# One schedule for all engines, searched anew: another order, other buffers, other ties, and four gated tiles in older buffers

## The chip, the cores and the metric

The kernel runs on one core of a Trainium2 chip. The metric is the time of one execution in microseconds (us) as the device counts it; lower is better. The core has five instruction queues: TensorE (PE, matmuls, with its weight loads shown apart as PEld), VectorE (DVE), ScalarE (ACT), GpSimd (POOL) and SyncE (SP), which only issues transfers. POOL issues some transfers as well. Each queue runs its instructions in the order in which the program puts them; queues wait for each other by semaphores.

## What is computed

Inputs are q, k and v of shape (4, 8, 768, 64) and three weight matrices. Attention picks, for each query, 6 of the chunks of 32 keys by an upper bound on the scores, and a gated layer follows.

```python
ub = sum(max(q * k_min, q * k_max))            # per query and chunk of 32 keys
ub = where(causal by chunk, ub, -1e9)
sel = the 6 chunks of largest ub, per query
scores = where(sel and causal, q @ k.T / 8, -1e9)
attn = softmax(scores) @ v                     # 8 heads, concatenated to x: (3072, 512)
gate = 1 / (1 + exp(-(x @ w_gate)))            # (3072, 1536)
out = (gate * (x @ w_val)) @ w_out             # (3072, 512)
```

## The kernel before

**Stages.** The 24 blocks of 128 rows (4 batches of 6) are dealt to eight units, u0 to u7, of three blocks each. u0 has the first blocks of batches 0 to 2, which need no choice of chunks and are computed apart ("first", names with f, as kf16_2, scf_2, expf_2_0, cmf_2_1, pvf_2_1, xf_2_1, xpsf_2_1, xTf_2_1: cast of keys, scores, exponential, causal select, values, normalised rows, their turn on PE, and its copy into xT). For u1 to u7 a stage prepares (turns q and k, takes extremes of k by chunk, bounds ub on PE, picks the sixth largest with MAX8, spreads the verdict as rows of a mask into hq), a stage attends (per head: score pieces sc on PE, exponentials exp on ACT, causal selects cm on POOL, values pv on PE, rows x on DVE), and ffn does the gated layer: 12 products g and 12 products v of 128 columns of the hidden layer each, a tanh on ACT (gate), the product of both on DVE (hg, six tiles of two column blocks a unit), then the product with w_out. In u5 to u7 part of the gate products, and in u4 to u7 the last product, are done by seven products in place of eight, with sums of blocks on DVE and POOL ahead (ss, tt, tw, sw, sx) and sums of the results on DVE behind (c11, c12, c21, c22 and so on).

**Order by hand.** Nothing in the kernel decides an order when it is built. The function declares 2010 operations with the engines on which each may run and the buffers that it reads and writes. Three long strings then fix the rest. ORDER lists all operations with an engine for each (P, A, V, G, S for PE, ACT, DVE, POOL, SP), and they are issued in that order, so each engine's own queue is the list cut down to its letter. SLOTS gives each buffer a number among those of its kind (for instance 8 banks ps of the accumulator memory, 6 tiles v, 9 tiles hg, 2 tiles osb); a buffer waits until the last user of the one that lay there before is done. TIES lists pairs a<b: operation a, on POOL, also waits for the end of operation b, on DVE, though it reads nothing of it. Durations written in the declarations (pool, dve, act, pe) were the search's input and do nothing when the kernel is built.

**Names in the prediction.** Weights come by POOL's queue as ten transfers: wgp (the first quarter of rows of the first third of w_gate's columns, L610), wg0 (the rest of that third, L612), wg1 and wg2 (the other thirds), wv0 to wv2 (L613) and wo0 to wo2 (L618). g_u0_0 to g_u0_3 read wgp and wg0, g_u0_4 to 7 read wg1, g_u0_8 to 11 read wg2. hkp... are copies of a fixed pattern into the mask rows of the keys (64 rows by 1536 columns), which may run on POOL, ACT or DVE; fl_0 to fl_29 are 30 matmuls of ones whose results nobody reads (L591). hk0/hk1 and hq0/hq1 of a unit are halves of keys and queries copied to where the score pieces read them; kx0/kx1 are the extremes (L681), kcr the ranges (L688), kt a cast of the turned keys. All plain copies stand on L452 (ACT), L454 (DVE) and L456 (POOL), the helper copy.

The lines that carry out an order:

```python
for op in plan.order():
    n = len(traced)
    op.emit(op.engine)
    for b in ties.get(op.name, ()):
        tc.add_manual_dep(traced[n], ends[b], ...)
    ends[op.name] = traced[-1].name
```

Of the kernel before, what the change touches and what calls it, by code (L numbers as in the profile page):

```python
# [108 lines left out]
qf_u1_2=V v11=G wv1=G wg1=G hq0_u1_3=G qT_u1_0=P kt_u1_3=A hk0_u1_3=G hq1_u1_3=G wv2=G xTf_2_1=A xTf_2_0=A qf_u1_0=A qm_u1_0=A
g_u0_0=P g_u0_2=P kx0_u1_3=V kcr_f=V kcr_u1=V hkp101=V hq1_u1_0=V hkf1=V kt_u1_1=V hk0_u1_1=G wg2=G qm_u1_2=A qm_u1_1=A ub_u1=P  # L110
ubn0_u1=V ubm0_u1=V hq0_u1_1=A hq0_u1_2=A g_u0_3=P g_u0_1=P mx0_u1=V ap0_u1=V apt0_u1=V hqm0_u1_0=V v_u0_1=P v_u0_0=P v_u0_2=P
hq0_u1_0=A tanh_u0_2=A tanh_u0_1=A hg_u0_1=V ubn1_u1=V v_u0_3=P tanh_u0_3=A hg_u0_3=V ubm1_u1=V hg_u0_2=V tanh_u0_0=A hg_u0_0=V
hk0_u1_0=A hq1_u1_1=A sc_u1_0_2=P exp_u1_0_2=A sc_u1_1_2=P sc_u1_0_1=P sc_u1_0_0=P exp_u1_1_2=A sc_u1_1_0=P sc_u1_1_1=P
exp_u1_0_0=A exp_u1_0_1=A v_u0_7=P wo0=G hqm0_u1_2=G sc_u1_2_2=P exp_u1_2_2=A sc_u1_2_0=P exp_u1_2_0=A sc_u1_3_0=P sc_u1_3_2=P
exp_u1_3_2=A exp_u1_1_0=A sc_u1_3_1=P exp_u1_3_1=A exp_u1_3_0=A v16_0_3=G wo1=G v_u0_4=P sc_u1_2_1=P v_u0_6=P exp_u1_2_1=A
hk1_u1_0=G v16_0_2=G wo2=G mx1_u1=V ap1_u1=V apt1_u1=V hqm1_u1_0=V g_u0_5=P tanh_u0_5=A v_u0_5=P exp_u1_1_1=A hqm1_u1_2=A g_u0_6=P
tanh_u0_6=A g_u0_7=P tanh_u0_7=A hg_u0_7=V v16_0_1=G cm_u1_3=G pv_u1_3=P cm_u1_2=G hk1_u1_1=G g_u0_4=P tanh_u0_4=A hg_u0_4=V
vf1_3=G hq1_u1_2=G pv_u1_2=P sc_u1_5_1=P sc_u1_4_2=P sc_u1_4_1=P rz_u1_1=V x_u1_1=V exp_u1_4_1=A v_u0_9=P v_u0_10=P xps_u1_1=P
xT_u1_1=A exp_u1_4_2=A hg_u0_6=V hk1_u1_3=V hg_u0_5=V v_u0_8=P g_u0_10=P tanh_u0_10=A kcr1=V hg_u0_10=V g_u0_8=P tanh_u0_8=A
hg_u0_8=V sc_u1_5_2=P exp_u1_5_2=A g_u0_9=P tanh_u0_9=A hg_u0_9=V sc_u1_4_0=P exp_u1_4_0=A cm_u1_1=G pv_u1_1=P cm_u1_0=G qn_u2_2=G  # L120
sc_u1_5_0=P pv_u1_0=P exp_u1_5_0=A sc_u1_6_1=P exp_u1_6_1=A sc_u1_6_2=P exp_u1_6_2=A exp_u1_5_1=A sc_u1_7_2=P sc_u1_7_0=P
g_u0_11=P qT_u2_2=P sc_u1_7_1=P tanh_u0_11=A exp_u1_7_2=A exp_u1_7_0=A exp_u1_7_1=A kn_u2_1=V kT_u2_1=P rz_u1_0=V x_u1_0=V
xps_u1_0=P cm_u1_5=G pv_u1_5=P cm_u1_4=G pv_u1_4=P qf_u2_2=V q1_u2=S qn_u2_1=V qT_u2_1=P sc_u1_6_0=P kt_u2_1=A exp_u1_6_0=A
kn_u2_0=G kT_u2_0=P kt_u2_0=A v_u0_11=P rz_u1_2=V xT_u1_0=V x_u1_2=V xps_u1_2=P q3_u2=S qn_u2_3=G qT_u2_3=P cm_u1_7=G pv_u1_7=P
kx0_u2_0=V o0_u0_0=P o1_u0_0=P hg_u0_11=V kx1_u2_1=V kx1_u2_0=V cm_u1_6=G pv_u1_6=P rz_u1_3=V x_u1_3=V q0_u2=S qn_u2_0=A qT_u2_0=P
o0_u0_1=P xps_u1_3=P xT_u1_3=V qf_u2_1=A hq0_u2_2=A qf_u2_3=A qm_u2_1=G hq1_u2_1=G k2_u2=S kn_u2_2=G hk1_u2_0=A xT_u1_2=A
kT_u2_2=P k3_u2=S kn_u2_3=A kT_u2_3=P qf_u2_0=V hq0_u2_1=G hq0_u2_0=G qm_u2_0=G hk0_u2_1=G o2_u0_0=P osb_u0_0=A hq1_u2_0=A
qm_u2_2=A qf0_3=S qfT_3=P o1_u0_1=P o2_u0_1=P vf_3=S kf1_3=S kf0_3=S kfT_3=P v_0_5=S v_0_4=S kx0_u2_1=V kx0_u2_3=V kx1_u2_3=V
kx1_u2_2=V kx0_u2_2=V qm_u2_3=V kcr_u2=V ub_u2=P qf16_3=V kt_u2_3=A kf16_3=V osb_u0_1=A scf_3=P expf_3_0=A out_u0_0=S vc_3=G
hk1_u2_1=G hk0_u2_0=V hk0_u2_3=G kt_u2_2=A g_u1_1=P tanh_u1_1=A hk0_u2_2=A g_u1_0=P tanh_u1_0=A o0_u0_2=P expf_3_1=A cmf_3_0=G  # L130
pvf_3_0=P o1_u0_2=P ubn1_u2=V ubn0_u2=V mx1_u2=V ap1_u2=V apt1_u2=V hqm1_u2_0=V sc_u2_4_0=P exp_u2_4_0=A sc_u2_4_2=P exp_u2_4_2=A
sc_u2_5_0=P sc_u2_5_1=P sc_u2_5_2=P exp_u2_5_2=A sc_u2_4_1=P exp_u2_4_1=A cmf_3_1=G pvf_3_1=P mx0_u2=V rzf_3_0=V ap0_u2=V xf_3_0=V
# [269 lines left out]
def kernel(  # L402
# [17 lines left out]
    T = 384  # L420
# [1036 lines left out]
```

## Time and profile before

| | us |
|---|---|
| median of three runs | 281.94 |
| lowest and highest of them | 281.69, 282.36 |
| the profiled execution | 281.46 |
| its span, first to last instruction | 279.8 |

| engine | busy us | of the span | instructions |
|---|---|---|---|
| PE | 269.8 | 96% | 2806 |
| PEld | 190.0 | 68% | 2806 |
| DVE | 232.1 | 83% | 686 |
| ACT | 180.5 | 65% | 386 |
| POOL | 163.3 | 58% | 262 |

Busy is the time in which at least one instruction of the engine runs. Matmuls overlap each other, and their ends are modelled, so PE's pace is read from the starts of its matmuls rather than from their durations. In timelines a row begins with its start and its length in us; a bracket behind a row gives the engine's idle time before it and what ended it, as far as the semaphores tell. In the view of transfers the last number is the time from issue to landing.

### The profile page before, as it was taken

The numbers are of one execution on the slowest core, as the hardware profiler recorded it, in microseconds if no ns is written. First come the engines' busy times: TensorE is split into PE (matmuls) and PEld (weight loads), VectorE is DVE, ScalarE is ACT, GpSimd is POOL, SyncE is SP. The second block draws the span as 40 slices with busy tenths as digits, with TensorE's granted clock in tenths as the row PEclk, the third lists the DMA queues.
The fourth block names the chain that finished last, engine by engine and source line by source line (L and its number), as shares of the span: only waits on it lengthen the run. The fifth ranks groups of instructions, "written<-read, shape, count | busy, mean of one in ns | idle before, by whom it ended". The sixth has DMA issues, their size and how long they took to land.

```text
span 279.8 us, 7565 instructions
## 1 busy us (share of the span) xinstructions
PE 269.8 (96%) x2806; PEld 190.0 (68%) x2806; DVE 232.1 (83%) x686; ACT 180.5 (65%) x386; POOL 163.3 (58%) x262
## 2 busy tenths in 40 slices
PE   5879999999999999999999999999999999999995
PEld 3655658667755766556687657766888688778684
DVE  4789845786998998886999987878879998888875
ACT  6178868669957943559689988997983422341430
POOL 5697744639464781633759966724766477163441
PEclk9999999999999999999999999999999999999999
DMA  6999999999999598887986230100310033000304
GB/s 161 252 264 201 211 215 204 202 184 191 180 228 189 150 177 178 177 150 134 174 144 113 60 92 16 40 0 2 74 76 2 1 82 127 2 1 2 150 2 151
DMA packets 131717, 34.70 MB, mean 124 GB/s; under 512 B 119776, under 2 KB 128736, under 8 KB 131680
## 3 DMA queue, kind: packets, MB, share of 16 engines
q1 hardware_dynamic: 126912, 29.50, 50.3%
q0 software_dynamic: 4768, 4.72, 10.2%
q8 instruction: 22, 0.36, 0.5%
q14 instruction: 15, 0.12, 0.1%
HBM read 30.67 MB, written 6.29 MB: 132 GB/s over the span
## 4 chain that ended last, share of the span: by engine, by line
PE 84%; DVE 7%; DMA 6%; issue 1%; SPq 1%; POOL 0%; DVEq 0%
PE v_u L1259 20%; PE g_u L1259 15%; PE sc_u L957 12%; PE o_u L1308 11%; PE p_u L1082 8%; PE pv_u L990 7%; DMA wg<-in_moe_w_gate_dram 5%; PE p_g_u L1191 5%; PE ube_u L896 3%; DMA kf<-in_k_dram 1%; DVE ox L1099 1%; DVE xf L768 1%; DVE sw L1099 1%; DVE kcr L681 1%; DVE kx_u L681 1%
## 5 line engine op out<-in xcount | busy, mean ns | idle before, releaser
L968 ACT ACTIVATE att_u<-sc_u 128x512 f16<-128x512 f32 (+3 forms) x184 | 86.9, 570 | 8.6 <-PE sc_u L957 7.3
L1259 PE MATMUL v_u<-xT_u,wv 128*128 128x384 f16 x384 | 72.4, 326 | 0.0
L1280 DVE SCALAR_TENSOR_TENSOR hg_u<-gate_u,v_u 128x384 f16<-128x384 f16 x96 | 51.2, 545 | 19.0 <-ACT gate_u L1271 9.4
L1271 ACT ACTIVATE gate_u<-g_u 128x384 f16<-128x384 f32 x72 | 35.1, 498 | 40.1 <-PE g_u L1259 35.0
L1259 PE MATMUL g_u<-xT_u,wg 128*128 128x384 f16 x288 | 55.9, 326 | 1.0 <-ACT xT_u L452 0.6
L1259 PEld LDWEIGHTS <-wv 128*128 128x128 f16 x384 | 36.2, 98 | 20.3 <-issue 0.2
L974 POOL TENSOR_SCALAR_AFFINE_SELECT att_u<-att_u 128x384 f16<-128x384 f16 (+1 forms) x56 | 28.1, 512 | 37.4 <-ACT att_u L968 16.5
L1259 PEld LDWEIGHTS <-wg 128*128 128x128 f16 x288 | 26.8, 98 | 18.1 <-issue 1.6
L1308 PE MATMUL o_u<-wo,hg_u 128*128 128x512 f16 x144 | 34.3, 379 | 0.0
L990 PE MATMUL pv_u<-v,att_u 128*128 128x65 f16 x640 | 26.3, 193 | 0.0
L990 PEld LDWEIGHTS <-att_u 128*128 128x128 f16 x640 | 24.2, 98 | 2.9 <-issue 0.6
L1228 DVE TENSOR_TENSOR f_g_u<-p_g_u,f_g_u 128x192 f32<-128x192 f32 (+1 forms) x72 | 25.0, 384 | 1.0 <-PE p_g_u L1191 0.4
L957 PE MATMUL sc_u<-hqe,hke 128*128 128x128 f16 (+2 forms) x220 | 25.1, 243 | 0.0
L957 PE MATMUL sc_u<-hqo,hko 128*128 128x128 f16 (+2 forms) x220 | 24.1, 243 | 0.0
L1308 PEld LDWEIGHTS <-hg_u 128*128 128x128 f16 x144 | 13.7, 98 | 13.4
L957 PEld LDWEIGHTS <-hke 128*128 128x128 f16 x220 | 16.5, 98 | 4.9 <-issue 0.6
L957 PEld LDWEIGHTS <-hko 128*128 128x128 f16 x220 | 16.4, 98 | 4.4
L673 POOL CAST v<-v 128x512 f16<-128x512 f32 x23 | 14.2, 619 | 6.3 <-DMA v<-in_v_dram 2.3
L1271 ACT ACTIVATE gate_u<-f_g_u 128x384 f16<-128x384 f32 x24 | 11.9, 519 | 5.6 <-DVE hg_u L1280 2.9
L1011 DVE TENSOR_TENSOR x_u<-pv_u,rz_u 128x384 f16<-128x384 f32 (+1 forms) x28 | 14.6, 524 | 0.9 <-DMA xT_u<-x_u 0.5
L1099 DVE SCALAR_TENSOR_TENSOR sw<-p_u,sw 128x256 f32<-128x256 f32 (+1 forms) x20 | 10.6, 529 | 3.0 <-PE p_u L1082 1.8
L919 DVE MAX8 mx_u<-ubn_u 128x8 f32<-128x8 f32 (+16 forms) x152 | 12.7, 159 | 0.3
(187 smaller groups left out, 508.2 us busy)
## 6 DMA issues: line engine op xcount, KB each, us to landing
v<-in_v_dram SPq DMA_DIRECT2D x23, 256.0 KB, 4.3
k<-in_k_dram SPq DMA_DIRECT2D x12, 384.0 KB, 5.4
q<-in_q_dram SPq DMA_DIRECT2D x12, 384.0 KB, 5.6
out_dram<-osb_u SPq DMA_DIRECT2D x12, 256.0 KB, 3.2
out_dram<-sw SPq DMA_DIRECT2D x8, 256.0 KB, 2.1
wv<-in_moe_w_val_dram POOLq DMA_DIRECT2D x3, 512.0 KB, 9.1
wo<-in_moe_w_out_dram POOLq DMA_DIRECT2D x3, 512.0 KB, 17.4
qf<-in_q_dram SPq DMA_DIRECT2D x8, 128.0 KB, 3.1
```

Of the source, the lines that this page charges most:

```text
L957: nc.tensor.matmul(at(t)[:, o:o + 128 * m], hk[b % 2][e_][:, p, 128 * jb:128 * jb + 128], hq[u.side][e_][:, p, 128 * x:128 * (x + m)], sta ...
L968: plan.add(f"exp_{u.name}_{h}_{y}", {ACT: act(n)}, lambda e, t=t, att=att, b0=b0, n=n: nc.scalar.activation(at(att)[:, b0:b0 + n], at(t), ...
L974: nc.gpsimd.affine_select(out=dv, in_=dv, compare_op=ALU.is_ge, fill=0.0, base=0, pattern=[[0, u.m], [1, 128]], channel_multiplier=-1)
L990: nc.tensor.matmul(at(pv)[:, last, x, :], at(att)[:, c:c + 128], v16[b % 2][:, jb, h, :], start=(jb == 0), stop=(jb == ib))
L1011: plan.add(f"x_{u.name}_{p}", {DVE: dve(u.t)}, lambda e: nc.vector.tensor_tensor(at(x_).rearrange("p a (e d) -> p e a d", e=2), at(pv)[:, ...
L1082: nc.tensor.matmul(at(to)[:, side], a(j)[:, i], b(j)[:, i], start=j == i == 0, stop=j == 2 and i == 1)
L1099: plan.add(f"{p}_{name}", {DVE: dve(256 * n)}, lambda e: nc.vector.scalar_tensor_tensor(four()[:, lo], at(src) if n == 1 else at(src)[:, 0 ...
L1228: plan.add(f"{p}_{name}", {POOL: pool2(192 * n), DVE: dve(192 * n)} if slow else {DVE: dve(192 * n)}, lambda e: both(e).tensor_tensor(dst( ...
L1259: nc.tensor.matmul(at(t), w16[:, c, 128 * fb:128 * fb + 128], at(u.xt)[:, c, :], start=(c == 0), stop=(c == 3))
L1271: plan.add(f"tanh_{u.name}_{fb}", {ACT: act(T, not seven[0])}, lambda e, gv=gv, gate=gate: nc.scalar.activation(at(gate), gv(), AF.Tanh, s ...
L1280: plan.add(f"hg_{u.name}_{fb}", {DVE: dve(T)}, lambda e, vv=vv, gate=gate, hg=hg, fb=fb: nc.vector.scalar_tensor_tensor(at(hg)[:, fb % 2], ...
L1308: nc.tensor.matmul(at(o), at(hgs[fc // 2])[:, fc % 2, 128 * tb:128 * tb + 128], wo16[:, fc, lo:hi], start=(fc == 0), stop=(fc == NFB - 1))
```

## The change

ORDER, SLOTS and TIES are replaced as a whole. The 2010 operations are the same ones, and the sets of PE's and SP's operations too; 144 operations go to another engine among DVE, ACT and POOL (counts of operations: DVE 540 and 540, ACT 385 and 402, POOL 256 and 239). Ties go from 137 to 115. In the code three things change: the cast of keys k16 is marked port=True, which the search reads and the built kernel doesn't; the gated tiles hg_u7_2 to hg_u7_5 get kinds osb and v instead of hg (LATE); and at() lays such a tile over the 1024 half-width columns of that buffer, which has 512 columns of 32 bits.

```diff
@@ at()
+        if b.tile is None and b.kind in ("v", "osb") and b.name.startswith("hg_"):
+            b.tile = land.tile([128, 1024], F16, tag=f"{b.kind}{b.slot}", name=b.name)[:, 0:2 * T].rearrange("p (i t) -> p i t", i=2)
@@ keys_blocks()
-                     lambda e, p=p, k16=k16: copy(e, at(k16), at(raw)[:, p]), reads=every, writes=[k16], prio=next_())
+                     lambda e, p=p, k16=k16: copy(e, at(k16), at(raw)[:, p]), reads=every, writes=[k16], port=True, prio=next_())
@@ ffn()
+    LATE = {(7, 2): "osb", (7, 3): "osb", (7, 4): "v", (7, 5): "v"}
...
-                hgs.append(Buf("hg", f"hg_{u.name}_{fb // 2}", [128, 2, T], F16))
+                hgs.append(Buf(LATE.get((u.i, fb // 2), "hg"), f"hg_{u.name}_{fb // 2}", [128, 2, T], F16))
@@ ORDER, its begin
-ident=G ones16=V fl_4=P fl_2=P fl_8=P fl_3=P fl_1=P fl_0=P fl_29=P k2_u1=S kn_u1_2=A qf1_0=S kf1_0=S kf0_0=S fl_6=P fl_5=P epat0=V
-ap0=V epat=G hkp110=A hkp000=A hkp001=V kT_u1_2=P kcr0=V kt_u1_2=V hk0_u1_2=G vf1_1=G hkp011=V hkp010=G vf1_2=G hkp100=G kf1_2=S
...
+k2_u1=S ident=G kn_u1_2=A ones16=V fl_2=P fl_6=P fl_7=P fl_9=P epat0=V epat=G hkp000=G hkp001=A hkp011=G fl_3=P fl_13=P fl_5=P
+fl_11=P fl_8=P fl_10=P fl_0=P fl_4=P hq1=V ident16=V kT_u1_2=P kt_u1_2=V kf0_0=S kf1_0=S kfT_0=P kf16_0=A kcr0=V kxf0=V kxf1=V
```

Cut to one engine, the parts of the new order that the prediction uses are these (names as above).

```text
POOL before: ident epat hk0_u1_2 vf1_1 hkp010 vf1_2 hkp100 v10 v16_0_0 cmf_0_0 cmf_0_1 wgp cmf_1_0 vc_1
             cmf_1_1 hkf0 wg0 wv0 cmf_2_0 vc_2 kn_u1_3 cmf_2_1 kn_u1_1 v11 wv1 wg1 ...
POOL after:  ident epat hkp000 hkp011 vf1_2 hkp010 v10 hkp110 v16_0_0 vf1_1 cmf_0_0 cmf_0_1 hkp100 cmf_1_0
             vc_1 cmf_1_1 wg0 cmf_2_0 wgp kcr_f wv0 qn_u1_0 cmf_2_1 wv1 hk0_u1_0 wg1 qn_u1_2 qm_u1_1 wv2
             hkp101 wg2 hk0_u1_3 hq1_u1_2 wo0 hqm0_u1_2 wo1 v16_0_2 wo2 hk1_u1_0 hqm1_u1_0 v16_0_3 cm_u1_3
             hq1_u1_3 v16_0_1 cm_u1_2 hk1_u1_1 hq1_u1_1 cm_u1_0 ...
DVE after:   ... rzf_2_1 xf_2_1 xTf_0_0 kx1_u1_3 qf_u1_1 kx0_u1_0 xTf_2_1 kt_u1_3 kx1_u1_1 kx0_u1_1 kcr_u1 ...
PE before:   ... v_u0_8 g_u0_10 g_u0_8 sc_u1_5_2 g_u0_9 sc_u1_4_0 pv_u1_1 sc_u1_5_0 pv_u1_0 sc_u1_6_1 sc_u1_6_2 ...
PE after:    ... g_u0_6 sc_u1_5_0 sc_u1_5_1 sc_u1_5_2 sc_u1_4_1 sc_u1_4_2 v_u0_9 sc_u1_4_0 pv_u1_0 v_u0_10
             sc_u1_6_2 sc_u1_6_1 xps_u1_1 pv_u1_1 v_u0_8 g_u0_8 g_u0_10 g_u0_9 ...
ties after:  v16_0_2<hg_u0_2 hk1_u1_0<ap1_u1 cm_u1_2<hg_u0_5 hq1_u1_1<hg_u0_7 hqm1_u1_2<hg_u0_4 ...
```

535 lines of the change are left out of this document (266 added, 269 removed).

## The prediction

> **What bounds the kernel now.** First the page: shares of the engines, then the chain that ended last.
>
> ```profile
> span 279.8 us, 7565 instructions
> ...
> PE 269.8 (96%) x2806; PEld 190.0 (68%) x2806; DVE 232.1 (83%) x686; ACT 180.5 (65%) x386; POOL 163.3 (58%) x262
> ...
> PE 84%; DVE 7%; DMA 6%; issue 1%; SPq 1%; POOL 0%; DVEq 0%
> PE v_u L1259 20%; PE g_u L1259 15%; PE sc_u L957 12%; PE o_u L1308 11%; PE p_u L1082 8%; PE pv_u L990 7%; DMA wg<-in_moe_w_gate_dram 5%; PE p_g_u L1191 5%; PE ube_u L896 3%; DMA kf<-in_k_dram 1%; DVE ox L1099 1%; DVE xf L768 1%; DVE sw L1099 1%; DVE kcr L681 1%; DVE kx_u L681 1%
> ```
>
> PE carries the chain, but one transfer, a gate weight, has 5% of it (14 us). Busy time by stretches, cut where PE has a gap, shows where idle time is left (columns: length, then busy us and instructions of PE, PEld, DVE, ACT, POOL, clock, DMA share, GB/s).
>
> ```profile
> 0.00:27.00 27.00, 20.94 (x179) 14.39 (x180) 20.39 (x50) 17.10 (x31) 19.55 (x36) 1.00 1.01 220
> 27.00:41.24 14.24, 14.24 (x120) 9.11 (x116) 9.62 (x42) 10.78 (x27) 8.52 (x16) 1.00 1.21 213
> 41.80:273.00 231.20, 231.20 (x2484) 163.76 (x2485) 197.90 (x589) 152.30 (x329) 133.81 (x209) 1.00 0.53 106
> ```
>
> From 41.80 to 273 PE has no gap, and its matmuls are the same 2806 after the change: nothing can be won there, only lost. What can be won lies in the head, in the one gap at 41 us, and in the tail. PE's order of time and the chain of waits:
>
> ```profile
> 24.32 0.48 PE L1259 MATMUL g_u<-xT_u,wg 128*128 128x384 f16 x2 [0.57 <-ACT xT_u L452]
> 24.32 0.26 PEld L1259 LDWEIGHTS <-wg 128*128 128x128 f16 x2 [0.74 <-DMA wg<-in_moe_w_gate_dram]
> ...
> 34.79 0.81 PE L1259 MATMUL g_u<-xT_u,wg 128*128 128x384 f16 x4
> ...
> 40.59 0.81 PE L1259 MATMUL v_u<-xT_u,wv 128*128 128x384 f16 x4
> 41.80 1.48 PE L1259 MATMUL g_u<-xT_u,wg 128*128 128x384 f16 x8 [0.40 <-DMA wg<-in_moe_w_gate_dram]
> ```
>
> ```profile
> 27.68 14.07 DMA wg<-in_moe_w_gate_dram
> ```
>
> So three landings of gate weights time PE: the first two (one queue, needed by g_u at 24.32, whose last xT copy ends at the same moment), the third (g_u0_5 at 34.79), the fourth, issued at 27.68 and landed at 41.75. Eight matmuls of 384 columns take 1.31 us from start to start (41.80 to the score piece at 43.11, below), 0.1635 each, so after the four at 40.59 PE was free at 41.24: the wait for the fourth weight is 0.56 us. (The row says 0.40 idle, since it lets the pipeline's end run on.)
>
> **The change part by part.**
>
> *The fourth gate weight (wg2).* The first product that reads it was g_u0_10; now it is g_u0_8, and five score pieces (sc_u1_5_0, 5_2, 4_0, 6_2, 6_1) and two groups of nine value matmuls (pv_u1_0, pv_u1_1) stand ahead of it that stood behind; no op left that stretch. Rows for them:
>
> ```profile
> 43.11 0.27 PE L957 MATMUL sc_u<-hqo,hko 128*128 128x256 f16 x1
> 43.22 0.81 PE L1259 MATMUL g_u<-xT_u,wg 128*128 128x384 f16 x4
> 43.87 0.39 PE L957 MATMUL sc_u<-hqo,hko 128*128 128x128 f16 x4
> 44.09 0.44 PE L990 MATMUL pv_u<-v,att_u 128*128 128x65 f16 x9
> 44.37 0.39 PE L957 MATMUL sc_u<-hqo,hko 128*128 128x128 f16 x4
> ```
>
> By starts: 0.11 for 256 columns, 0.22 for four of 128, 0.28 for nine values, 0.16 for 384 columns. Two 256s, two fours, one 384, two nines: 0.22 + 0.44 + 0.16 + 0.56 = 1.38 us. PE gets there at 41.24 + 1.38 = 42.62, 0.87 after the landing of 41.75. The wait goes whole: **-0.56**. It would come back only if that landing were over 0.87 late against PE.
>
> *The head.* Two things end before the first g_u. (a) The last xT copy. Its source is the last causal select of the first blocks, on POOL. Rows (POOL, then ACT, then DVE):
>
> ```profile
> 2.98 0.98 POOL L566 TENSOR_SCALAR_AFFINE_SELECT epat<-epat 32x768 f16<-32x768 f16 x1
> ...
> 7.89 1.46 POOL L456 COPY hke<-epat 64x1536 f16<-64x1536 f16 x1
> 13.66 0.80 POOL L610 DMA_DIRECT2D wg<-in_moe_w_gate_dram  x1
> 17.29 0.80 POOL L612 DMA_DIRECT2D wg<-in_moe_w_gate_dram  x1
> 18.09 0.78 POOL L613 DMA_DIRECT2D wv<-in_moe_w_val_dram  x1
> 19.47 0.62 POOL L456 CAST vh<-vf 128x512 f16<-128x512 f32 x1
> 20.02 0.51 POOL L456 COPY kn_u<-kq_u 128x384 f32<-128x384 f32 x1
> 20.48 0.63 POOL L753 TENSOR_SCALAR_AFFINE_SELECT attf<-attf 128x512 f16<-128x512 f16 x1
> 22.53 0.75 POOL L612 DMA_DIRECT2D wg<-in_moe_w_gate_dram  x1
> ```
> ```profile
> 23.62 0.65 ACT L452 COPY xT_u<-xpsf 128x256 f16<-128x256 f16 x2
> ```
> ```profile
> 21.96 0.42 DVE L768 TENSOR_TENSOR xf<-pvf,rzf 128x256 f16<-128x256 f32 x1
> 22.31 0.55 DVE L454 COPY qf_u<-qT_u 128x384 f32<-128x384 f32 x1
> 22.77 0.55 DVE L681 TENSOR_REDUCE kx_u<-kT_u 128x12 f32<-128x384 f32 x1
> ```
>
> Before, from wg0's issue (17.29) to that select's end (21.11) is 3.82 us. Now POOL has wg0, a select, wgp, the small kcr_f, wv0, a cast and the select: 0.80 + 0.63 + 0.80 + 0.3 + 0.78 + 0.51 + 0.63 = 4.45, less six overlaps of 0.05, 4.15. Ahead of wg0, POOL now has five pattern copies of 1.46 (two before), four selects of 0.63, two casts of 0.62 and three memsets (an estimate of 0.5): 7.3 + 2.5 + 1.2 + 0.5 = 11.5 us from 3.96, where the pattern ends, less fourteen overlaps of 0.05. That is 14.8 with no wait, and 17.29 if it waits as before. I take 15.8, a wait of 1.0 for the first exponentials. The select ends at 15.8 + 4.15 = 20.0 to 20.4, as the third block's scores allow. From its end to the last xT copy it was 24.27 - 21.11 = 3.16; now it is 1.28 to the end of xf (21.11 to 22.38) and behind it on DVE one xT copy, two extremes, one qf copy and the last xT copy (0.47 apart for the three, 0.3 for the two), 2.0: 3.3. xT is ready near 23.6, between 23.3 and 24.4.
> (b) The weights. The small first piece (wgp) now goes after wg0:
>
> ```profile
> wg<-in_moe_w_gate_dram POOLq DMA_DIRECT2D x1, 384.0 KB, 6.8
> wg<-in_moe_w_gate_dram POOLq DMA_DIRECT2D x1, 128.0 KB, 5.6
> ```
>
> It was 13.66 + 5.6 and 17.29 + 6.8 = 24.09. Now wgp is issued between 17.5 and 18.5, so it lands between 23.1 (5.6 later) and 25.3 (6.8 later). The engines were full all this time (share 1.01, then 1.21), and the same 512 KB go through, so I take 24.0. First g_u at 24.1: **-0.2**, bounds -1.0 and +1.0.
> What this start can bring is capped: wg1, issued at 22.53, took 12.0 us
>
> ```profile
> wg<-in_moe_w_gate_dram POOLq DMA_DIRECT2D x1, 512.0 KB, 12.0
> ```
>
> and landed at 34.53, 0.26 ahead of g_u0_5, which keeps its place in PE's work. Beyond 0.26, a start gained earlier becomes a wait there, unless the weights come earlier too.
>
> *Ops moved between engines.* 144 small ops change engine. At the mean duration of each kind on its new engine, POOL loses 43.6 us and gets 34.3, DVE loses 20.2 and gets 19.5, ACT loses 17.9 and gets some 28. None of the three is the bound from 41.80 on (197.90, 152.30 and 133.81 busy of 231.20), so **0**, hidden beside PE's matmuls; without that cover, ACT's 10 us more would be paid, at most in full.
>
> *SP's queue.* The loads of unit 1 end one issue later (24th, was 23rd) and unit 2's come one earlier: inside the bounds of (a), **0**.
>
> *Ties* (POOL's waits for a DVE end) fall from 137 to 115: **0** taken, a gain excluded by the gapless PE; the loss is a rival below.
>
> *Four gated tiles of unit 7* lie in buffers whose raw values and outputs were read some units earlier. What they waited for before (tiles of units 5 and 6) costs nothing now, since PE shows no gap to 273: **0**.
>
> *The tail.* The last six products, their evictions and the three last stores stand in the same order: **0**.
>
> ```profile
> 275.81 1.66 SPq L1127 DMA_DIRECT2D out_dram<-ox  x3
> ```
>
> Sum: -0.56 - 0.2 = -0.76 against the profiled 281.46 (span 279.8 and 1.7 around it): 280.7. The median of the runs, 281.94, is 0.48 above that execution: **281.2**.
>
> **The rivals.**
> *Slower: POOL becomes the bound of the first 38 us.* Before:
>
> ```profile
> 3.97:38.90 34.93, 30.74 (x270) 21.13 (x271) 26.72 (x82) 24.92 (x52) 25.40 (x43) 1.00 1.14 230
> ```
>
> Now sc_u1_5_0 (PE needs it some 14.2 us after the first g_u, at 38.3, six us earlier than before) reads hq1_u1_1, which is POOL's 47th op: 45 ops after the pattern, 31.9 us by durations, 29.4 less overlaps of 0.055, so 33.4 with no wait. Before, POOL idled 9.5 us of that stretch; with all of that again hq1 ends at 42.9, 4.6 late. Of the waits 3.3 were for kt_u copies that now feed ACT instead:
>
> ```profile
> L456 POOL COPY hke<-kt_u 64x384 f16<-64x384 f16 x3 | 1.7, 559 | 3.3 <-DVE kt_u L454 3.3
> ```
>
> That leaves 6.2 at most, 1.3 late. I take 4.2 of waits (1.0 for exponentials, the rest for the DVE ends that it is tied to), 37.6, 0.7 in time. Queued behind it are the causal selects that pv_u1_0 and pv_u1_1 read. It decides from a lateness of 1.3 on (0.76 + 0.56); at 40.4, 2.1 late, the time is 281.2 + 2.1 = 283.3. Against it: what POOL waits for is PE's and DVE's work, which comes earlier too.
> *Slower by blocked copies.* DVE and POOL hold each other up here:
>
> ```profile
> 8.04 1.39 DVE L597 CAST ident<-ident 128x128 f16<-128x128 f32 x1
> ...
> 200.95 0.35 DVE L1171 TENSOR_TENSOR hke<-xT_u 128x384 f16<-128x384 f16 x1
> 201.54 0.94 DVE L1171 TENSOR_TENSOR hke<-xT_u,hke 128x384 f16<-128x384 f16 x1
> ```
>
> The cast ends at 9.43, just after POOL's copy (7.89 + 1.46 = 9.35), and of two like subtractions one takes 0.59 longer. With 22 ties fewer, three such stretches on PE's chain among the paired sums of units 5 to 7 cost 1.8: 281.2 + 1.8 = 283.0. Against it: PE ran gapless past this one. [...]
> *No change: wgp lands last.* At 25.3, first g_u comes 1.0 late; the 0.56 at 41 us still goes: 281.94 + 1.0 - 0.56 = 282.4. A new wait of half a us anywhere gives the same verdict.
> *More.* If the weights come 0.5 earlier with POOL's earlier issues, the cap rises and the start of 23.6 is paid out: -0.56 - 0.7: 280.7.
>
> **How the numbers follow.** Forecast 0.45, more 0.10, no change 0.22, POOL 0.15, blocked copies 0.08. A change under 0.2% (0.56 us) can't be told from none: faster is below 281.38. Of the forecast nine tenths are faster: 0.40 + 0.10 = 0.50; same 0.05 + 0.22 = 0.27; slower 0.23. The forecast's own range is 280.8 to 281.6 (start -0.6 to +0.2). To 280.0 it takes in the start's bound (281.94 - 0.56 - 1.0 = 280.4) and the scatter of the runs shown (0.67 wide), to 283.0 no change and half of the slower cases.
>
> **What would show it.** The idle before g_u L1259 for the gate weight near 41 us gone; first g_u between 23.6 and 24.4; PE without a gap from there to 273. Wrong: a first g_u after 24.6 with the weight load waiting for its DMA; PE gaps at sc_u L957 behind POOL's hqo copies near 38 us; DVE adds of over 0.6 us ahead of gaps at p_u L1082.

## The result, and the profile after

| | before | after |
|---|---|---|
| median of 22 executions each, us | 281.71 | 285.15 |
| lowest and highest | 280.60, 282.73 | 282.33, 287.01 |
| ratio, 95% interval | 1 | 1.0102 (1.0079 to 1.0125) |
| the profiled execution | 281.46 | 282.39 |

The changed kernel is 1.0% slower; forecast were 281.2 us and a gain. The ratio leaves out the changed kernel's slowest execution, which ran in a slower state (the means are then 284.58 and 281.71 us); the medians are 1.2% apart. Its profiled execution is one of its fastest, so the traces of its later executions count as well. First the page: span, engines, the granted clock by slices, and the chain that ended last.

```profile
span 280.7 us, 7561 instructions
...
PE 269.6 (96%) x2806; PEld 189.9 (68%) x2806; DVE 231.8 (83%) x686; ACT 191.9 (68%) x403; POOL 153.3 (55%) x245
...
PEclk9977999999999999999999999999999999999999
...
PE 92%; DMA 3%; DVE 1%; SPq 1%; ACT 1%; issue 1%; POOL 0%; DVEq 0%; ACTq 0%
```

The gate weight's 5% of the chain is gone, as forecast, and PE has 92% instead of 84%; yet the span is 0.9 longer. The view of stretches (length, then busy us and instructions of PE, PEld, DVE, ACT, POOL, clock, DMA share, GB/s) still shows no idle PE from 41.80 on, and in the head a mean clock of 0.87, where it shows 1.00 for the kernel before:

```profile
0.00:27.00 27.00, 19.98 (x179) 13.85 (x180) 18.13 (x45) 18.54 (x34) 24.32 (x38) 0.87 1.01 218
27.00:41.24 14.24, 14.24 (x127) 9.48 (x126) 9.13 (x38) 11.32 (x27) 11.05 (x20) 1.00 1.21 215
41.80:273.00 231.20, 231.20 (x2469) 163.14 (x2468) 200.58 (x596) 161.50 (x343) 115.86 (x186) 1.00 0.53 106
```

Where the time went is read from three marks in every trace: the start of the ninth matmul of the first products (g_u0_3, once the bounds of unit 1 are through PE), the end of PE's last matmul, the end of the span. Two profiles of the kernel before and four of the changed one, all unaltered:

| profile | first g_u | ninth | ninth to PE's end | PE's end to span's end | span |
|---|---|---|---|---|---|
| before | 24.32 | 26.95 | 249.31 | 3.49 | 279.75 |
| before, again | 23.75 | 26.86 | 249.34 | 3.51 | 279.71 |
| after | 23.91 | 26.95 | 249.72 | 4.02 | 280.68 |
| after, second | 25.60 | 28.24 | 250.14 | 4.04 | 282.43 |
| after, third | 24.94 | 27.58 | 250.05 | 4.03 | 281.66 |
| after, fourth | 24.34 | 27.26 | 249.71 | 4.05 | 281.02 |

On the means the changed kernel loses 0.60 us ahead of the ninth matmul (between 0.0 and 1.3), 0.58 from there to PE's end although the wait of 0.56 is gone, and 0.53 behind PE's last matmul: 1.7 in all. These four executions took 282.4 to 284.1; what the others, up to 287, lose beyond that is taken up with the clock below.

**The middle.** The two rows of each of the next fences are the same work in both kernels: eleven value matmuls (pv_u2_0), then a product. Start and length, before and after:

```profile
67.48 0.50 PE L990 MATMUL pv_u<-v,att_u 128*128 128x65 f16 x11
67.82 0.65 PE L1259 MATMUL g_u<-xT_u,wg 128*128 128x384 f16 x3
```
```profile
67.39 0.63 PE L989 MATMUL pv_u<-v,att_u 128*128 128x65 f16 x11
67.85 0.65 PE L1260 MATMUL g_u<-xT_u,wg 128*128 128x384 f16 x3
```

From start to start it was 0.34 us and is now 0.46. Between two of the eleven lie 0.117 us too much, where PE waits for a causal select on POOL (cm_u2_0) that ends 0.06 before PE goes on. No view calls it idle: the modelled end of a value matmul lies 0.19 behind its start, so a shorter wait hides under it. Read from the starts, the first profile of after has nine such gaps from 31 us on: four behind POOL (pv_u1_2 0.127, sc_u1_5_0 0.116, pvf_3_1 0.111, pv_u2_0 0.117), two among the scores of unit 1 (0.135, 0.083), three late (0.125, 0.099, 0.082), 0.995 in all, where before has one of 0.098. At each of the five that aren't behind POOL, PE goes on some 0.05 us after the end of an instruction on DVE. The second and third profile have one more, of 0.41 and 0.35, in the bounds of unit 3 at 84 us.

**The tail.** The groups of the kernel's last line, before and after: engine, instruction, count, ns shortest/median/longest, first and last start.

```profile
L1452 POOLq EVENT_SEMAPHORE  x4: 17/17/17, 279.0 to 279.6; - x4
L1452 SPq DRAIN  x3: 7/7/7, 278.9 to 279.2; - x3
```
```profile
L1453 POOLq EVENT_SEMAPHORE  x4: 17/17/17, 279.9 to 280.6; - x4
L1453 SPq DRAIN  x3: 7/7/124, 279.4 to 280.2; - x3
```

SP's first drain here comes within 0.1 us of the landing of the last store in both (278.84 and 279.33). From it to POOL's answer it was 0.1 us and is 0.5: SP stands still for 0.38 between its first drain and the second, which itself takes 124 ns instead of 7.

**The head.** In the second profile of after, the chain and PE's order of time:

```profile
17.61 7.94 DMA wg<-in_moe_w_gate_dram
```
```profile
23.53 0.55 PE L794 MATMUL qT_u<-ident,qn_u 128*128 128x128 f32 x3 [0.15 <-POOL qn_u L455]
25.60 1.47 PE L1260 MATMUL g_u<-xT_u,wg 128*128 128x384 f16 x8 [1.51 <-DMA wg<-in_moe_w_gate_dram]
...
28.24 0.50 PE L1260 MATMUL g_u<-xT_u,wg 128*128 128x384 f16 x2
```

The small piece wgp, now behind wg0, lands last, at 25.55, and PE waits 1.51 us for it. In the four profiles it lands at 23.87, 25.55, 24.89 and 24.29. What passed beside it stands in the view of transfers for 21 to 24 us (queue, packets, MB, share of 16 engines), before and in the second profile of after:

```profile
q0 software_dynamic: 521, 0.52, 112.7%
q1 hardware_dynamic: 104, 0.03, 6.5%
```
```profile
q1 hardware_dynamic: 1687, 0.43, 70.3%
q0 software_dynamic: 277, 0.26, 51.9%
```

q0 carries POOL's weights, q1 SP's loads. Before, the weights had the engines nearly to themselves in these 3 us (0.52 MB); after, half of that went through (0.26 MB), while the 256-byte packets of SP's loads (1687 in 0.43 MB, v_0_2 among them) passed at the same time. The two shares, 70.3% and 51.9%, show both queues served side by side; but before, a load of q1 (v_0_1, issued at 16.07, landing at 31.51) was under way in the same 3 us and q1 had 6.5%, so no fixed split between the two queues is shown.

### The profile page after: what moved, and what is told of

It is laid out like the page before. It is cut to its first block, busy times and chain, and to the rows that moved or that the text cites. A ratio compares the mean times of both kernels' runs of the same rounds, so it can differ in the third digit from the quotient of the medians.

```text
span 280.7 us, 7561 instructions
## 1 busy us (share of the span) xinstructions
PE 269.6 (96%) x2806; PEld 189.9 (68%) x2806; DVE 231.8 (83%) x686; ACT 191.9 (68%) x403; POOL 153.3 (55%) x245
## 4 chain that ended last, share of the span: by engine, by line
PE 92%; DMA 3%; DVE 1%; SPq 1%; ACT 1%; issue 1%; POOL 0%; DVEq 0%; ACTq 0%
PE v_u L1260 22%; PE g_u L1260 17%; PE sc_u L956 13%; PE o_u L1309 11%; PE p_u L1081 9%; PE pv_u L989 7%; PE p_g_u L1190 5%; PE ube_u L895 3%; DMA vf<-in_v_dram 2%; PE qT_u L794 1%; DMA qf<-in_q_dram 1%; DVE ox L1098 1%; PE kT_u L794 1%; SPq L635 1%; PE ubo_u L895 0%
## 5 line engine op out<-in xcount | busy, mean ns | idle before, releaser
L967 ACT ACTIVATE att_u<-sc_u 128x512 f16<-128x512 f32 (+3 forms) x184 | 86.0, 566 | 4.8 <-PE sc_u L956 4.3
L1281 DVE SCALAR_TENSOR_TENSOR hg_u<-gate_u,v_u 128x384 f16<-128x384 f16 x96 | 50.5, 544 | 19.8 <-ACT gate_u L1272 9.7
L1260 PE MATMUL g_u<-xT_u,wg 128*128 128x384 f16 x288 | 56.8, 327 | 0.0
L989 PE MATMUL pv_u<-v,att_u 128*128 128x65 f16 x640 | 27.4, 193 | 0.0
L989 PEld LDWEIGHTS <-att_u 128*128 128x128 f16 x640 | 24.9, 98 | 3.2 <-issue 0.6
L1227 DVE TENSOR_TENSOR f_g_u<-p_g_u,f_g_u 128x192 f32<-128x192 f32 (+1 forms) x72 | 25.6, 383 | 0.7
L956 PE MATMUL sc_u<-hqe,hke 128*128 128x128 f16 (+2 forms) x220 | 24.6, 243 | 0.0
L956 PE MATMUL sc_u<-hqo,hko 128*128 128x128 f16 (+2 forms) x220 | 24.6, 243 | 0.0
L1309 PEld LDWEIGHTS <-hg_u 128*128 128x128 f16 x144 | 13.7, 98 | 13.4
L1068 POOL TENSOR_TENSOR sw<-hg_u,hg_u 128x256 f16<-128x256 f16 x10 | 6.9, 691 | 25.3 <-DVE hg_u L1281 17.2
```

The costliest lines, as they stand in the source:

```text
L956: nc.tensor.matmul(at(t)[:, o:o + 128 * m], hk[b % 2][e_][:, p, 128 * jb:128 * jb + 128], hq[u.side][e_][:, p, 128 * x:128 * (x + m)], sta ...
L967: plan.add(f"exp_{u.name}_{h}_{y}", {ACT: act(n)}, lambda e, t=t, att=att, b0=b0, n=n: nc.scalar.activation(at(att)[:, b0:b0 + n], at(t), ...
L989: nc.tensor.matmul(at(pv)[:, last, x, :], at(att)[:, c:c + 128], v16[b % 2][:, jb, h, :], start=(jb == 0), stop=(jb == ib))
L1227: plan.add(f"{p}_{name}", {POOL: pool2(192 * n), DVE: dve(192 * n)} if slow else {DVE: dve(192 * n)}, lambda e: both(e).tensor_tensor(dst( ...
L1260: nc.tensor.matmul(at(t), w16[:, c, 128 * fb:128 * fb + 128], at(u.xt)[:, c, :], start=(c == 0), stop=(c == 3))
L1281: plan.add(f"hg_{u.name}_{fb}", {DVE: dve(T)}, lambda e, vv=vv, gate=gate, hg=hg, fb=fb: nc.vector.scalar_tensor_tensor(at(hg)[:, fb % 2], ...
```

## The experiments

Theories: W or D (weights and loads share one budget of transfers in the head, and the new order puts the wrong bytes first), C (the halved clock), P (DVE and POOL hold each other up), M (small waits on PE), T (the stall in SP's end). L and S are variants for single loads. "After" and "before" name the base of each edit; lines of edits are parts of the order, as in the change.

**1. The changed kernel again** (a_again; later a_ref and a_third).

> The changed kernel, unaltered, profiled once more: its first profiled execution (282.39 us) was among the fastest of 22 (median 285.15), so the missing 2.8 us are not in that trace. Theory C (clock): the granted clock is 0.5 for at least one stretch of 6.8 us that begins between 14 and 28 us, and if the execution is near 285 the stretch lies later, over the products that begin near 24 us, whose pace is then 0.32 a matmul instead of 0.16. Rival P (POOL and DVE hold each other up by chance): clock stretch as in the first trace (17.7 to 24.6), and the difference shows as PE gaps behind DVE or POOL after 25 us. Rival W (weights): landings of wg or wv later than 24, 27.3, 30.6, 34.2, 38.0, 41.7 and PE gaps there.

> The changed kernel, unaltered, timed beside the three below on one chip: 284 to 286, with the first g_u wherever wgp lands (23.9 and 25.6 in its two profiles so far).

> The changed kernel, unaltered, once more. Theory D: first g_u at 24.5 to 26 us behind wgp; the gaps at pv_u1_2, sc_u1_5_0, pvf_3_1 and pv_u2_0 as in all its profiles, 0.4 us between SP's last two drains; 283 to 286.

Measured: 284.14 us; 283.65 (four executions, 1.0103, 1.0061 to 1.0146); 282.73; the last two are just below what was expected. P has little here: one gap of 0.25 in the bounds of unit 1 (a_third). W's landings are late in three of four, as shown above, and PE waits for them. The clock was halved for 6.8 us in all four, but from between 15.2 and 17.7 us on, so ahead of all but the first products; that C's stretch lies over the products was a miss.

**2. The kernel before again** (b_again).

> The kernel before, unaltered, profiled again. Theory D: first g_u at 23.0 to 24.5 us, the last of wgp and wg0 landing within 0.5 of it; the same waits later (0.1 us at 39, the fourth weight near 41), last drain of SP right behind the one before it; 280.5 to 282.

Measured: 281.42; all points but one hold (first g_u 23.75, the ninth matmul at 26.86). wg0 lands at 24.33, 0.58 behind the first g_u instead of within 0.5; by the starts PE waits 0.47 us for it. The two profiles of before differ by 0.1 at the ninth matmul, the four of after by 1.3.

**3. Fillers in PE's gaps** (after).

```diff
+fl_30=P ... fl_45=P pvf_1_0=P
+fl_46=P ... fl_49=P xpsf_1_1=P
+fl_50=P ... fl_53=P pvf_2_0=P
+fl_54=P ... fl_57=P qT_u1_3=P
+fl_58=P fl_59=P qT_u1_1=P
```

> The changed kernel with 30 more fillers (matmuls of ones that nobody reads) in PE's gaps of the first blocks: 16 ahead of pvf_1_0 (a gap of 2.5 us at 12.6), 4 each ahead of xpsf_1_1, pvf_2_0 and qT_u1_3, 2 ahead of qT_u1_1. No other operation moves. Theory C: the clock is not halved any more (1.00 from about 4 us on), and the time falls from 285.2 to between 280.8 and 282.3. Rivals P and W: no change, 284.5 to 286, since PE only gets work that nobody waits for; if the fillers are in the way, up to 1 us more.

Measured: 289.5 us, 1.0288 (1.0261 to 1.0315); a bad experiment, not a verdict on C. PE's order of time:

```profile
13.05 5.17 PE L592 MATMUL fl<-ones 128*128 128x256 f16 x16
18.06 0.29 PE L761 MATMUL pvf<-vh,attf 128*128 128x65 f16 x4
```

Sixteen fillers take 5.0 us at a clock of 1.00, 0.33 each: all write one accumulator bank. Eight of after's own, each in another bank, start 0.11 apart from 5.86 us on, so in one bank each seems to wait for the one before. The sixteen held up pvf_1_0 by some 2.8 us.

**4. One load earlier; fillers of before bunched** (a_vf1 on after, b_bunch on before).

```diff
+vf_1=S kf1_2=S q0_u1=S k0_u1=S
-kf1_2=S q0_u1=S k0_u1=S vf_1=S
```
```diff
+fl_5=P fl_23=P fl_21=P fl_20=P epat0=V
+fl_7=P fl_25=P fl_28=P fl_27=P fl_22=P fl_24=P kx0_u1_2=V
```

> The changed kernel with one load, vf_1, issued three places earlier on SP (ahead of kf1_2, q0_u1 and k0_u1, nearly where the kernel before has it). It landed at 14.42, PE waited 2.3 us for its cast. Theory C: the wait shrinks by about 1.5 us, but the clock is still halved in most executions, so 283.5 to 285.5. Rival L (the late load is itself what is lost): all that follows comes 1 to 1.5 earlier, 283.7 to 284.2 with the clock's stretch left as it is.

> The kernel before, with eight of its 30 fillers moved from 16 to 21 us to the front, as the changed kernel has them: three more ahead of kT_u1_2, five more behind kfT_0. Nothing else moves. Theory C: the clock warms earlier and is halved again for 6.8 us somewhere between 14 and 30 us, the time rises from 281.7 to between 282.5 and 285.5. Rivals P, W and L: 281.4 to 282.0.

Measured: 283.4 us, 1.0082 (1.0059 to 1.0104), not to be told from after, the first g_u still at 25.25 behind wgp; and 281.55, 1.0006 (0.9994 to 1.0019). In b_bunch the clock is halved from 17.0 to 23.8 us, as in after, and the time does not move: a halved clock that ends before the products costs nothing here. That is the first blow to C.

**5. The order of the weights, both ways** (a_wgp on after, b_wgp on before), and cleaner fillers (a_fill2, a_wgp_fill2).

```diff
+cmf_0_1=G wgp=G hkp100=G
-cmf_2_0=G wgp=G
```
```diff
-cmf_0_1=G wgp=G
+wg0=G wgp=G wv0=G
```
```diff
+fl_30=P ... fl_47=P pvf_1_0=P
+fl_48=P ... fl_51=P pvf_2_0=P
+fl_52=P ... fl_55=P qT_u1_3=P
+fl_56=P ... fl_59=P pvf_2_1=P
+fl_60=P ... fl_65=P g_u0_2=P
```

> The changed kernel with wgp (the small first piece of the gate weight) issued on POOL ahead of hkp100, near 11.8 us, instead of behind wg0 and cmf_2_0, at 17.6. Theory W (weights): PE's first product waits for the later of wg0 and wgp; both start 2 us later than before and meet the 256-byte packets of v_0_2, so in the second profile of the changed kernel wgp landed at 25.55. Moved, wgp lands before 19, wg0 by 23.3 to 24.6, the first g_u starts at 23.9 to 24.7, and the time falls from 285.2 to 282.6 to 284.0 (POOL's later copies come 0.8 later, at most 0.3 of it paid). Theory C (clock): the time stays at 284.5 to 285.5, whenever the weight lands.

> The kernel before with one move: wgp behind wg0 on POOL (issued near 17.3 instead of 13.7). Theory W: wgp lands last, at 24.8 to 25.8, the first g_u starts 0.6 to 1.4 us later, the wait for the fourth gate weight at 41 us shrinks by up to 0.5, and the time rises from 281.4 to 281.9 to 282.8. Theory C: 281.2 to 281.7, nothing changes for the clock.

> The changed kernel with 36 more fillers, this time turned over several accumulator banks so that none waits for the one before it (in a_fill all of a place shared a bank and stood 0.33 to 0.43 us apart): 18 ahead of pvf_1_0, 4 each ahead of pvf_2_0, qT_u1_3 and pvf_2_1, 6 ahead of the first product g_u0_2. Theory C: no half clock between 10 and 28 us, and the time falls from 285.2 to 282.5 to 284.0, with less scatter. Theory W: the first g_u still waits for wgp until 25.2 to 25.6 us; 284.0 to 285.2.

> Both edits together. If W and C both hold, what is left against the kernel before is some 0.9 us of waits of 0.1 us each on PE after 30 us and 0.4 us in SP's last drain, less the 0.56 us wait that went: 281.6 to 282.6. Theory W alone: as a_wgp. Theory C alone: as a_fill2.

Measured: a_wgp 283.62, 1.0096 (1.0058 to 1.0135), wgp landing at 17.13, wg0 at 23.98, first g_u at 24.41: the landing moved as W has it, the time did not measurably. Its one trace shows a reason: the ninth matmul starts at 27.94, later than in three of the four profiles of after, since something else now ends last. The copy hkp101, one of the 144 moved operations, stands on POOL instead of DVE. There it runs beside kcr_u1 on DVE, the ranges that the bounds of unit 1 need, and kcr_u1 takes 1.39 us instead of the 0.21 of a_again, where the two don't overlap. Rows of POOL, DVE and PE in a_wgp, then DVE in a_again:

```profile
25.66 1.46 POOL L454 COPY hke<-epat 64x1536 f16<-64x1536 f16 x1
25.80 1.39 DVE L686 TENSOR_TENSOR kcr<-kx_u,kcr 128x48 f32<-128x48 f32 x1
...
27.24 0.45 PE L894 MATMUL ube_u<-qm_u,kcr 64*32 64x320 f32 x1 [0.66 <-DVE kcr L686]
```
```profile
24.86 0.21 DVE L687 TENSOR_TENSOR kcr<-kx_u,kcr 128x48 f32<-128x48 f32 x1
```

By the starts PE waits 0.87 us here. This is theory P in one direction, since POOL's copy takes the 1.46 us that it takes in the kernel before; no run put hkp101 back, so what it costs over many executions isn't known. In three of the four profiles of after kcr_u1 takes 1.38 us too, but the late weight hides all of it but 0.06, 0 and 0.25.

b_wgp 1.0014 (0.9978 to 1.0049), first g_u at 24.68 behind wgp: undecided. a_fill2 1.0072 (1.0037 to 1.0107) with a mean clock of 0.993 to 1.000 in the seven executions compared; the interval meets that of after, so C's gain isn't shown; its one profile shows a mean clock of 0.75 (358 us), so its landings can't be compared. a_wgp_fill2 1.0098 (1.0064 to 1.0132): a miss for both theories. Its weights land at 16.78 and 21.59, earlier than in any other profile of after's order (the next is 23.29, below), but ACT now waits for unit 1's queries (view of waits for ACT, 18 to 25 us: line, releaser, us, times, longest):

```profile
ACT qn_u L454 <- DMA kq_u<-in_q_dram: 2.1, 1, 2.1
```

and the first g_u starts at 26.90. These queries were issued at 13.81, as in a_wgp (13.82), and landed at 21.09 instead of 18.55, which fits theory D: what is given to one queue is taken from the other. But part of the delay is the experiment's own. The last six fillers stand right ahead of the first product and take from 25.61 to 26.90, since the clock was halved at 24.55.

**6. SP's order** (a_sp and a_sp_wgp on after, b_sp_wgp on before).

```diff
-vf_2=S v_0_3=S q1_u1=S k1_u1=S q2_u1=S
+vf_2=S q1_u1=S k1_u1=S q2_u1=S v_0_3=S
```
```diff
+vf_2=S q1_u1=S v_0_3=S k3_u1=S q0_u1=S k1_u1=S
+wg0=G wgp=G wv0=G
```

> The changed kernel with one load moved on SP: v_0_3 (1024 packets of 256 bytes) behind q2_u1, so that unit 1's q and k are all issued ahead of it, as the kernel before has it. Theory D (the transfers of the head are one budget: what PE waits for at 24 us is the last of unit 1's q and k, turned and copied, and of wg0 and wgp, and each byte put ahead of them costs): unit 1's loads land about 1 us earlier, the transposes end earlier, the weights stay where they are, so the first g_u is still set by wgp; 284 to 285. Theory S (only unit 1's loads matter): first g_u near 24.0, 283 to 284.

> v_0_3 behind q2_u1 and wgp ahead of hkp100: both orders as in the kernel before. Theory D: first g_u between 23.6 and 24.5, 282.0 to 283.2; what then stays above the kernel before are waits of 0.1 us each on PE after 30 us (0.9 in all) and 0.4 us in SP's last drain, less the 0.56 us wait. Theory C (clock) says nothing new: 283 to 285.

> The kernel before with the two orders of the changed kernel: v_0_3 issued ahead of the last three loads of unit 1 (k3_u1, q0_u1, k1_u1), wgp behind wg0. Theory D: the first g_u starts at 24.8 to 26.0 instead of 24.3, the wait for the fourth gate weight shrinks, and the time rises from 281.3 to 282.2 to 283.5. Theory C: 281 to 281.8 unless the clock is halved longer.

Measured: a_sp 282.64, 1.0069 (1.0046 to 1.0092); a_sp_wgp 283.58, 1.0093 (1.0068 to 1.0117), though its first g_u starts at 24.72 and its ninth at 28.01: above D's bounds. Here too kcr_u1 takes 1.38 us beside hkp101, and by the starts PE waits 0.62 for it. b_sp_wgp 283.27, 1.0055 (1.0021 to 1.0089), first g_u behind the weight:

```profile
25.46 0.82 PE L1257 MATMUL g_u<-xT_u,wg 128*128 128x384 f16 x4 [1.07 <-DMA wg<-in_moe_w_gate_dram]
```

Its other loss is at later weights. By the starts PE waits 0.39, 0.54 and 0.50 us at 29.80, 36.88 and 43.84, the last two right behind the landings of the third and fourth gate weight (36.84, 43.80); that the wait for the fourth would shrink was a miss. So the two transfer orders of after, put into before, make it slower by 0.2 to 0.9%: that part is shown. Taken out of after, the order of v_0_3 gives back some 0.3% (a_sp against after), and the two intervals still meet; with wgp moved as well nothing is left of it.

The profile of a_sp fell on its slowest execution (284.89) and shows what the clock can cost. Stretches, then PE's order of time:

```profile
21.56:24.98 3.42, 1.70 (x13) 1.03 (x11) 3.39 (x10) 2.98 (x8) 3.17 (x5) 1.00 1.23 214
24.98:28.39 3.41, 3.03 (x16) 1.26 (x24) 1.58 (x2) 0.25 (x1) 3.30 (x5) 0.50 1.21 209
```
```profile
25.36 2.74 PE L1259 MATMUL g_u<-xT_u,wg 128*128 128x384 f16 x8 [2.03 <-DMA wg<-in_moe_w_gate_dram]
...
29.41 0.82 PE L1259 MATMUL g_u<-xT_u,wg 128*128 128x384 f16 x4
```

PE waits 2.03 us for the weight, the clock is halved, and the first eight matmuls take 2.74 us instead of 1.47; the ninth starts 4.05 behind the first, not 2.64. Here the stretch costs 1.4 us. Of the 22 executions of after, eleven have a mean clock of 0.982 or less and a median of 285.75; the other eleven, at 0.985 or more, have 283.68. The first profile of after has 0.988 with one halved stretch of 6.83 us, a_sp's has 0.982 with 3.41 us more. But a low mean alone does not decide: one execution of a_sp took 282.59 with 0.982, and one of a_wgp 283.64 with 0.979.

**7. Single terms** (b_wg2 on before, the others on a_sp).

```diff
+sc_u1_5_2=P exp_u1_5_2=A sc_u1_4_0=P exp_u1_4_0=A g_u0_10=P tanh_u0_10=A
```
```diff
+fl_30=P ... fl_47=P pvf_1_0=P
+fl_48=P fl_49=P pvf_2_0=P
+fl_50=P fl_51=P qT_u1_3=P
```
```diff
@@ a_sp_small, the first four in ORDER, and store()
+g_u0_6=P pv_u1_2=P
+v_u0_9=P sc_u1_5_0=P
+sc_u2_5_0=P pvf_3_1=P
+g_u1_3=P pv_u2_0=P
+        n = 2 if name in ("u0_0", "u0_1", "u0_2") else 1
...
-out[r:r + 128, lo:hi], src())
+[nc.sync.dma_start(out[r + i * 128 // n:r + (i + 1) * 128 // n, lo:hi], src()[i * 128 // n:(i + 1) * 128 // n]) for i in range(n)]
```

> The kernel before with two pieces of scores and their exponentials (sc_u1_5_2, sc_u1_4_0) moved ahead of g_u0_10, the first product on the fourth gate weight; nothing else. My prediction's step (the wait of 0.56 us goes whole where enough PE work stands ahead): 0.33 us of work stands ahead, so the wait falls to about 0.2 and the time by 0.3: 280.6 to 281.1 where the kernel before has 281.0 to 281.4, ratio 0.9985 to 0.9995. Rival: the later products come later by as much and lose it again; ratio 1.000.

> a_sp (v_0_3 behind q2_u1) with 22 more fillers over several banks: 18 ahead of pvf_1_0, two each ahead of pvf_2_0 and qT_u1_3. Theory C: clock 1.00 or halved for less than 4 us in most executions, and the time falls from a_sp's 282.6 by 0.3 to 1.0, to 281.6 to 282.3. Rival (the halved clock lies where PE waits anyway): 282.4 to 283.0.

> a_sp with four PE operations moved by one or a few places so that those that wait for POOL come later (g_u0_6 ahead of pv_u1_2, v_u0_9 ahead of sc_u1_5_0, sc_u2_5_0 ahead of pvf_3_1, g_u1_3 ahead of pv_u2_0), and three stores of unit 0 split in two, which gives SP 214 instructions in place of 211, as in the kernel before. Theory M (the small waits): the gaps at pv_u1_2, sc_u1_5_0, pvf_3_1 and pv_u2_0 (0.127, 0.116, 0.111, 0.117 us) go, 0.47 in all. Theory T (the end is a matter of how many instructions SP has): from the landing of the last store to the end 0.9 us, as in the kernel before, not 1.35. Both: 281.6 to 282.0, from a_sp's 282.6. Rival (the gaps move on to what comes next, the drain stays): 282.4 to 282.9.

> a_sp with only two of the four moves (sc_u2_5_0 ahead of pvf_3_1, g_u1_3 ahead of pv_u2_0). Theory M: the gaps at 61 and 67 us go and none comes, 0.22 us: 282.2 to 282.6, ratio to before 1.004 to 1.006. Rival: no change against a_sp, 282.6, ratio 1.006 to 1.007.

b_wg2: slower, 1.0033 (1.0009 to 1.0056). The wait for the weight is gone and two others stand in its place, for accumulator banks that ACT's exponentials free; by the starts they are 0.37 and 0.90 us:

```profile
41.23 0.49 PE L955 MATMUL sc_u<-hqo,hko 128*128 128x256 f16 x5 [0.20 <-ACT att_u L966]
42.46 0.97 PE L1257 MATMUL g_u<-xT_u,wg 128*128 128x384 f16 x5 [0.74 <-ACT att_u L966]
```

a_sp_fill3: 282.64, 1.0061 (1.0037 to 1.0084), mean clock 0.99 or more in nine of ten executions, one of 0.986: the same median as a_sp, but on another chip, where before has 281.34 instead of 280.92. The two ratios can't be told apart, so at the median no loss to the clock is shown. Its profile (clock 0.998, first g_u 24.22, ninth 27.21) still has 249.73 from the ninth to PE's end and 4.02 behind it, and 0.32 of waiting for kcr_u1 (1.47 us) ahead of the ninth.

a_sp_small: 283.95, 1.0089 (1.0067 to 1.0111), no gain over a_sp. The moves at 61 and 67 us took their gaps away; the two near 39 us made larger ones, as PE's order of time shows:

```profile
39.52 0.81 PE L1260 MATMUL v_u<-xT_u,wv 128*128 128x384 f16 x4 [0.31 <-ACT gate_u L1272]
...
41.62 0.43 PE L988 MATMUL pv_u<-v,att_u 128*128 128x65 f16 x9 [0.31 <-ACT att_u L966]
```

For T, the groups of its last line:

```profile
L1453 SPq DRAIN  x3: 7/7/7, 281.1 to 281.4; - x3
```

The stall between the drains is gone, but 0.37 us of standing still are now found between two of SP's last waits, three instructions earlier: three instructions more moved it by three. There it was exposed again; in the kernel before, a wait of 0.38 us at that same place (277.96 to 278.35) ends right behind the landing of the last store but one (278.33).

a_sp_two keeps the two good moves: 283.2 us, 1.0053 (1.0017 to 1.0089), not to be told from a_sp. In its trace both gaps are gone; the eleven value matmuls take 0.34 again. But the same trace has a wait of 0.46 for the third gate weight at 35.88 (landing 35.83), more than the 0.22 that they gave:

```profile
68.54 0.50 PE L988 MATMUL pv_u<-v,att_u 128*128 128x65 f16 x11
68.88 0.33 PE L955 MATMUL sc_u<-hqe,hke 128*128 128x256 f16 x2
```

No version was faster than the kernel before.

## Why the prediction was wrong

- *The fourth gate weight, -0.56.* The mechanism was right: the first product on it starts at 42.99 in the first profile, 1.30 behind the landing at 41.69 (forecast 0.87 behind), and no profile of after waits there. But b_wg2 shows that such a wait is not a sum to be cashed alone: work pulled ahead of it needs banks, and waited 0.37 and 0.90 us for those.
- *"From 41.80 to 273 PE has no gap", so moved ops, ties and tiles at 0.* This step failed, together with the cover that it lent to the 144 moved operations. The stretch reads 231.20 of 231.20 in both kernels, and still after has 0.9 us of new gaps from 31 us on. The row can't show a wait shorter than the modelled run-out of a matmul (0.19 us from the start of a value matmul, whose successor starts 0.03 behind it); I used it as proof of slack. By the starts, four of the nine gaps (0.47) are behind POOL and five (0.52) behind DVE. The rival "POOL becomes the bound" came true at the place that it named, sc_u1_5_0 behind hq1_u1_1 (which ends at 39.01, forecast 37.6), but by 0.1 us instead of 2.
- *The head, -0.2 (bounds -1.0 and +1.0).* The place was right (the landing of wgp), and POOL's issues came as forecast (wg0 at 15.4 to 15.9, wgp at 17.6 to 17.9). The size was not right: 24.0 was taken for the landing because "the same 512 KB go through"; four profiles gave 23.87 to 25.55, the first product 23.91 to 25.60, and the ninth matmul +0.60 on the mean. Two of the four first products lie in the forecast's 23.6 to 24.4, by the luck of the landing, and two behind 24.6, its sign of being wrong. The step that failed is holding the weights' share of the engines fixed while their first issue moved from 13.7 to 15.6 and SP's loads into the same microseconds (0.26 MB of weights in 3 us instead of 0.52). The rival "wgp lands last" was what happened; its price of 282.4 assumed the other zeros.
- *SP's queue, 0.* Not 0 together with the weights: b_sp_wgp shows 0.2 to 0.9% for both orders. How much of it is v_0_3's alone stays open.
- *The tail, 0.* The order of the last products is the same, but the end costs 0.53 more on the mean of four profiles, 0.38 of it a stall of SP that doesn't show in the kernel before, where a wait of 0.38 for a landing lies at its place. It goes with SP's instruction count, 211 instead of 214, in so far as a_sp_small's three more moved it by three; they did not take it away.
- *Four tiles in older buffers, 0; blocked copies.* No gap in the traces lies at a product that waits for those tiles. They were not tried alone. The rival of blocked copies was placed among the paired sums of units 5 to 7; it came in the head, where hkp101 went from DVE to POOL and kcr_u1 takes 1.38 us beside it. Its price was 0.06 us in the first profile and up to 0.87 where the weights came in time (a_wgp), so it is a second end of the head that the sum didn't have.
- *What was not in it.* The clock. At the median no cost is shown (a_sp_fill3 against a_sp), but in a_sp's profile it is 1.4 us. That the executions of after with a mean clock of 0.982 or less took longest is a coincidence in the records, not an experiment: in which of them the halved stretch lay over the products isn't known, and with it the cause of about half of the 3.4 us between the medians stays open.

By the sums: the profile that was forecast at 280.7 took 282.39, 1.7 more: 0.2 in the head, 1.0 in the middle (a gain of 0.56 turned into a loss of 0.4), 0.5 in the tail.

## What to carry to other kernels

An engine that the profile calls busy throughout is not proof of slack: compare the starts of equal groups of matmuls in two traces, since waits of 0.1 us behind another engine hide under modelled ends (0.19) and add up (0.995 in nine). In a stage that is bound by transfers, price a moved transfer by what else is on the engines in those microseconds, and expect scatter where two queues meet (23.87 to 25.55 for the landing of wgp in four profiles). A short wait taken away by reordering can come back as a wait for the buffers of the work that was pulled ahead (b_wg2: 0.37 and 0.90 us). And when one thing that ends last is moved ahead, look for the next one before the gain is counted: behind the weight stood kcr_u1 (0.87 us in a_wgp).

## What the runs showed of the hardware

The granted clock, in the first profile of after:

```profile
10.90:14.31 3.41, 1.90 (x27) 1.45 (x26) 2.38 (x7) 2.18 (x4) 2.98 (x4) 1.00 1.01 275
14.31:17.72 3.41, 1.70 (x25) 1.14 (x25) 1.93 (x8) 1.40 (x3) 2.89 (x5) 1.00 1.09 278
17.72:24.55 6.83, 6.02 (x34) 4.60 (x35) 6.14 (x18) 6.14 (x15) 6.63 (x11) 0.50 1.17 215
```

It was halved at 17.72 after two stretches of 3.41 us in which PE was busy 56% and 50% (its longest gap was 2.34 us), and full again at 24.55. In the kernel before, PE was busy 69% from 14.47 to 17.72, and the clock stayed at 1.00:

```profile
14.47:17.72 3.25, 2.24 (x33) 1.68 (x30) 2.97 (x9) 2.19 (x5) 2.71 (x5) 1.00 1.09 274
```

What decides between the two, these rows don't show. Nor does the view's 1.00 show the pace ahead of 14.47: there the fillers of the kernel before start 0.21 us apart from 1.31 to 13.33, those of after from 1.31 to 3.44 alone and 0.11 from 5.86 on.

Besides: fillers into one accumulator bank start 0.33 us apart (a_fill), over several banks 0.11 (after, from 5.86 us on), and 0.21 at the halved clock (a_wgp_fill2). A DVE operation of 0.21 us that begins 0.14 behind a POOL copy of 1.46 us takes 1.39 and ends 0.06 behind it (a_wgp). And SP stands still for 0.38 us between its first two drains in after (279.42 to 279.80), and for 0.37 three instructions earlier in a_sp_small, which has three more; what it does there no view names.
